# Selector-free attention for the groups from 6 on, and a new hand-written order of all steps

## The chip, the cores and the metric

The kernel runs on one core of a Trainium2 chip. The time is that of the device in microseconds (us), one launch, and the kernel before is given by the median of three runs. Five engines work from queues of their own, each in program order: PE (matrix multiply), DVE (vector), ACT (activation), POOL (GpSimd) and SP, which here only issues transfers. An engine goes on to its next instruction when the semaphores that this one needs have been raised, so one late instruction holds back all behind it on that engine.

## The reference

Linear attention with a feature map, followed by a two-layer MLP with an ELU in between. 8 batches of 8 heads, 576 positions, head size 64, 128 features; 4608 tokens of width 512; hidden width 2048.

```python
def phi(x):
    proj = np.einsum('bhsd,df->bhsf', x, w_phi)
    proj = proj - np.max(np.abs(proj), axis=-1, keepdims=True)
    return np.concatenate([np.exp(proj), np.exp(-proj)], axis=-1)
q_p, k_p = (phi(q), phi(k))
kv = np.einsum('bhsf,bhsd->bhfd', k_p, v)
z = np.sum(k_p, axis=2)
num = np.einsum('bhsf,bhfd->bhsd', q_p, kv)
den = np.einsum('bhsf,bhf->bhs', q_p, z)[..., None] + 1e-06
x = (num / den)            # then heads side by side: (4608, 512)
h = x @ w_in
g = np.where(h > 0.0, h, np.exp(np.minimum(h, 0.0)) - 1.0)
out = g @ w_out
```

With m the largest magnitude of a position's projection, the first half of its features is exp(proj - m) and the second exp(m - proj). So the two halves of a query's features carry different powers of exp(m), which do not cancel in the quotient, and m has to be applied somewhere.

## The kernel before

Four heads make a group (16 groups, two per batch). A group's k and q come in by a casting load (POOL queue, letters e, f, g for k, q, v), are transposed to feature-contraction layout (by PE for the first four groups, letters j to m; by a DMA transpose on the SP queue for the rest, letters n for k and o for q), and then run through these steps. A letter is a step of the order; a digit after it is the first PSUM bank it uses, a star puts it on the other of two engines.

- k side: A (`k_mm`, L267) three projections; B (`k_exp`, L278, ACT) both exponentials; C (`k_max`, L285, DVE) largest magnitude; D (`v_exp`, L295, ACT) and E, F (`v_scale`, `v_ones`, L304 and L313, POOL) scale v by the factor of each key; U (`kv_mm`, L477) and V (`kv_copy`, L487).
- q side: M (`m_mm`, L341) projects with positions on the partitions, N (`m_max`, L368, DVE) takes the largest magnitude. Then O (`m_split`, L394 and L395) splits it in two bf16 parts, P (`m_pe`, L401) transposes them, Q (`m_copy`, L406) copies them out of PSUM, and S (`q_mm`, L437) projects q again with features on the partitions; into the same banks L449 adds the maxima, by six matmuls with the 0/-1 selector matrix `sel` for each third. T (`q_exp`, L461, ACT) takes both exponentials.
- output side: W (`x_mm`, L526) multiplies by kv; both halves of the features add up in PSUM. X (`x_div`, L540, L541, L543, DVE) divides, and z (`x_dma`, SP queue) transposes the quotient into `xT`, the input of an MLP chunk, and into `xT_last`, which collects the ninth slot of 64 positions of all batches for the last chunk.
- MLP: nine chunks of 512 tokens. p (`h_mm`, L633) four matmuls of 512 columns; q (`h_exp`, L644, ACT); r (`h_min`, L649, POOL); s (`h_elu`, L653, DVE) writes `gT`; t (`o_mm`, L661) four matmuls of 512 columns into an output tile, four t to a tile; u (`o_copy`, L671) and v (`o_store`, L677).

No scheduler stands behind this: `ORDER` is one string of letters, and the loop at the end of the kernel pops, for each letter, the next argument of that step and issues its instructions. The order on every engine's queue, SP's and POOL's among them, is that of the string. `xT` has four buffers (`RING = 4`).

A second path is in the code and not taken: groups from `JOINED` on, and `JOINED` is 16. There, M makes ten places instead of nine (pieces of 4, 3 and 3), so that a query's maximum lies on the partition where its output row will be; w (`m_exp`) takes exp(m) and exp(2m) of it; S leaves the selector out; W writes the two halves of the features to separate banks in three pieces of 7, 7 and 6; x (`x_join`) multiplies the second half by exp(2m) and adds the first, R (`x_rec`) makes the reciprocal of the denominator, and y (`x_scale`) multiplies by it on POOL, or with a star on DVE. O, P, Q and X fall away. o issues two transposes of 64 partitions instead of one of 128.

Of the kernel before, what the change touches and what calls it, by code (L numbers as in the profile page):

```python
# [15 lines left out]


ORDER = """
eabeefgcj7dj6fkA0gk*CeA2A4CBj7CBl6Dkj1Bml0kDA6mEBM0CBA2ENBEBCl5l4BfmOBmhP7A0QM4BFES6NDBM2ETOCP5E
Q*TNU4FDFM6UBENj3V*S0kFEW4Tj7XU2hTUgkM4V*Y6NOM0Z*P7W2QNS4l7O*TXP6S0Q*Tl6mY3j2TZS4Tkj7mTW2kTp7XS0  # L20
qA4Tl6rsm*p3CTM6qNA0Bp2risBM6Cp3qp5qrl4Dsrm*Np2qp4qrsBA6Fsrp3CqqrBsrsEDsM4Bp2NM0Bp3NOM4qY7qrNp6r
W0eqZp5sFrsP7p4EqXQ*qS2rTsrS0sfM6Tsp5NETY4p3ZqEA6Tp2Cp4qrqU0BrsrsUqsBp5rVeS2qst7TrTA0p6CW2qsp4rB
stO*qXDrp6Bp5qsP1zW2qQrrsp4FsS0qXnp6Trp5EqzA2TtCrqEp1sDp0sBFtroEsBS4u*qp6EqTp7zU2TrrsUqsnqS4rV*r
p1ssW2zqTt7rsXop6A0qtTCrzM2sBW4NztBXp6M0qM2zA4NrtBgst1BNutCM2A6DM4NBFtO*fNBP3tQ*CM4S2t0u*TNTp7ED
S1qEA3S5TCtrTtEsToBU1FEp7TvBgA5UCqnO*p4V*rBW1szDp3qXvrtqsBW1rEp7sXp6qEA3u*qM1rnp5Brsp0qszBp7rNqp
6CzqrP2p1seqzsFp5rqDvrsp4qrsp7zqrsp6fsqvQ*rM0S2Esp5TNqt4rqrstTEsM0A2U6NFBrUO*BsS0tV*CTP7S5A2TotC
TW0QTt7XDBEW5zBS0XEtTzTA2S5CtTzu*BtTS0u*t4ToBM5tNTA2nM5BtNDBM0EA5tBCFp7EuNBU2FqOA0CUBnrp4VDzCM5q
p3NrBp2qsW0srqp7DsrgP6sp5qXQ*rp4qt6rszEsS0S2vTEp7Tzp5ETtqeTtfqM0qrS2NtrTosFTW0Frsp4EXp7qszrA0qU2
suUrvCM4V*p6szBW2Nqp7BXrp5qsp4rqsrA0qA2p6nsBrt7sBvOW4BCtzBXP1tqzDCrQ*A4S0EBzsM2TCtgTNFt6DBFu*EA0
S2BM4tfTCtETNtBEA2uM0U4eNBUBS6Vp1oTCA4Dp0TzFDp3qvqrp7qrvsBp6rsqW1sBrp0XqEnt3qsrtCEztsEW1zp7XrtO*  # L30
qsrM1M4u*p6sp3qNP7rp0qNQ*rt2sFS4M6TtNTtsqOp7rEsU3qS5A0rTtCTUsBS5Vp7Tou*Bp4vqW0qrP3p2vTQXrDp3zqsr
S0qst6zTrsp7TEszA4qS0CtzTrEsTM2ntNBFS0DA2ETtCoBt7EBW4gTtXFBU0zM2A4UNtV*vCuM0W2BzNtBXvt6uOzM0A2M4
NBtzNDP7tBEQCS0fA4TtBW2Tp7Xp1qCzrS2qt0u*EDzTstFBEvp7TFM4rqS2Np6ETosTU4rqUsA1rV*np3BsW4qCp7rteOqs
DP6rXtBp3uQszA1qM4S6NBzrp0TEsp5vCqEp4qTp3rBnrsW6qsp2qrXA0rp5Bszqp7sDrqp6CvFqrt4sBrzsqA2FS0sBrp5g
CtqsBtrETsS2M6Top5NETU0TM6UqNA2V*tODnCEW0up7BXrt6FqEszBP4W0DtQ*XFzEtzES0M2TtNrvTU4u*S0vM2UTNp6Tz
sV*M2S0NA4Tot7CTp3BA0tqCBrp2qsp5qrDp6rsqsBp4rqsW2qrtBXFrp5EszA0qM2sp6EBNzp4qrp3rsqOCtrqt5rsBsuP6
tsQ*M0A2S6NtTCDtTFEW0Bp7Xt6qzp4rsp1vqtrqzsBp7ru*ES2sqU4TrM0tNTUsA0S2Cp7VDtqEBp5u*O*TFp4rqp6srqTp
7rssP5W2Q*qt5XBrtqEszp4rW0zqA2p6CvtXDBEtqszp1Frp7rvsqEsut4zqrBtrvsU2sS0UTS5VTp7tqTrS0tTTp3u*TW5q
W0Xrp4st2zqsp7rXvtqsztrsp6zp7qtrqsp5rust6vqtrzsttp7p5qt4rqsp3rsp7qtrqsutrvsp6tt7uqtvrp5stqtrsp6t
5qp4rstqp6rsp3qp4rqstrqstrsp6t4qp3rsp2qp6rqsutrqvsp7rstqp6rsp3qup7rqvstrqsp6rsp5qt7rqsup3rvstqtr  # L40
stp6p5qp4rqst3rqstrsp6u*tqvp7rstqt6rusp5vp7qtrqsp4rsp5qp7rqstrqstrst5utvttt7utvttt6utvttt7u*tvtt
uv
"""


# [1 line left out]
def kernel(  # L47
# [178 lines left out]
    def new_t(name):  # L228
        return lambda: tpool.tile([P, NI, P], BF16, name=name + "T")
# [86 lines left out]
    def m_mm(n, c, bank=None):  # L316
        if n >= JOINED:
            v0, v1 = M_PIECES[c]
            pj = two_banks(bank).rearrange("p r (i f) -> p r i f", f=F)
            for v in range(v0, v1):  # L320
                for par in range(2):
                    hi, u = divmod(v, 5)
                    tpar, i0 = TILES[1][(2 * u + par) // 5][(2 * u + par) % 5]
                    assert tpar == par
                    rows = slice(par * D, (par + 1) * D)
                    nc.tensor.matmul(
                        pj[:, par, v - v0, :],
                        by_head(n)[rows, hi, i0 * D:(i0 + 2) * D],
                        w_sb[rows, :],
                        start=True,  # L330
                        stop=True,
                    )
            st["pm", n, c] = pj
            return
        own = min(n // FIRST, 1)
        p0, p1 = PIECES[own][c]
        pj = two_banks(bank).rearrange("p r (i f) -> p r i f", f=F)
        for j in range(p1 - p0):
            for par in range(2):
                rows = slice(par * D, (par + 1) * D)  # L340
                nc.tensor.matmul(  # L341
                    pj[:, par, j, :],
                    st["qT", n][rows, PLACE_OF[own][par][p0 + j], :],
                    w_sb[rows, :],
                    start=True,
                    stop=True,
                )
        st["pm", n, c] = pj

    def m_max(n, c):  # L350
        if n >= JOINED:
            v0, v1 = M_PIECES[c]
            mq = get(("mq", n), lambda: small.tile([P, 20], FP32, name="mx"))
            nc.vector.tensor_reduce(
                mq.rearrange("p (v r) -> p r v", r=2)[:, :, v0:v1],
                st["pm", n, c][:, :, 0:v1 - v0, :], axis=AX.X, op=ALU.max,
                apply_absolute_value=True,
            )
            return
# [8 lines left out]
        nc.vector.tensor_reduce(  # L368
            mq, st["pm", n, c][:, :, 0:p1 - p0, :], axis=AX.X, op=ALU.max,
            apply_absolute_value=True,  # L370
        )
# [37 lines left out]
    def q_mm(n, c, bank=None):  # L409
# [373 lines left out]
```

## Time and profile before

| | |
|---|---|
| median of 3 runs | 373.46 us (372.49 to 373.53) |
| the profiled execution, its own time | 373.46 us |
| its span, first to last instruction | 371.7 us |
| granted TensorE clock | 0.997 |
| PE busy | 349.8 us |
| ACT busy | 251.5 us |
| DVE busy | 244.7 us |
| POOL busy | 194.3 us |
| first matmul starts | 4.73 us |
| last matmul ends | about 367 us |
| DMA transposes of q, 12 | 1.31 us on the queue, 3.3 us to landing |
| DMA transposes of `xT_last`, 28 | 1.23 us on the queue, 3.1 us to landing |

The span is 1.76 us shorter than the time of that execution; this stands around the span and holds no instruction of the kernel. Rows of the profile give one instruction's duration from its start to its end; matmuls are pipelined, so a stream of them costs less per matmul than the row's mean.

### The profile page before, as it was taken

Reading aid. Unit: us, or ns where it says so; the run is one execution under the profiler, and the core shown is the slowest. Engines: PE = TensorE matmul, PEld = TensorE weight load, DVE = VectorE, ACT = ScalarE, POOL = GpSimd, SP = SyncE. Lnnn points to the kernel's source line nnn. Section 1 sums busy time; section 2 is a strip of 40 time slices with the busy share of each in tenths; the row PEclk is TensorE's granted clock in tenths of the full one; section 3 lists DMA queues with packets and bytes.
Section 4 is the critical chain, followed back from the end, with each engine's and each line's share of the span. In section 5 each row is a group of like instructions: output and inputs, shape, how many; then the busy total and the mean of one; then the engine's idle time right before and its main releaser. Section 6 shows DMA issues by size and latency. Waiting matters only on the chain.

```text
span 371.7 us, 9982 instructions
## 1 busy us (share of the span) xinstructions
PE 349.8 (94%) x4034; PEld 193.6 (52%) x4084; DVE 244.7 (66%) x425; ACT 251.5 (68%) x463; POOL 194.3 (52%) x307
## 2 busy tenths in 40 slices
PE   2798799999999999999999999999999999999994
PEld 1576576555465455554554555545555544444442
DVE  3968986867876868777767787777664632454400
ACT  2969798787789688955977898686566432453410
POOL 6762778267943775684544676464554332353400
PEclk9999999999999999999999999999999999999998
DMA  7997998689965699990679879620204212021223
GB/s 107 178 206 130 175 207 134 99 140 188 153 132 81 86 176 163 169 180 2 119 112 174 118 147 118 114 60 7 47 19 103 58 32 56 0 58 29 56 69 74
DMA packets 68158, 39.72 MB, mean 107 GB/s; under 512 B 48016, under 2 KB 62480, under 8 KB 68112
## 3 DMA queue, kind: packets, MB, share of 16 engines
q1 hardware_dynamic: 52176, 20.59, 31.8%
q0 software_dynamic: 15856, 18.35, 31.7%
q8 instruction: 32, 0.52, 0.6%
q14 instruction: 14, 0.11, 0.1%
q10 hardware_dynamic: 80, 0.13, 0.1%
HBM read 36.77 MB, written 9.44 MB: 124 GB/s over the span
## 4 chain that ended last, share of the span: by engine, by line
PE 82%; DVE 7%; ACT 3%; issue 3%; POOL 2%; DMA 1%; POOLq 0%; ACTq 0%
PE banks L661 32%; PE banks L633 29%; PE banks L477 5%; PE banks L526 5%; PE banks L437 3%; PE banks L341 2%; PE banks L267 2%; PE banks L449 2%; ACT EK L278 2%; DVE gT L653 2%; POOL e_sb L649 1%; DVE mk L285 1%; DMA kn<-in_k_dram 1%; DVE xp L543 1%; DVE mq L368 1%
## 5 line engine op out<-in xcount | busy, mean ns | idle before, releaser
L649 POOL TENSOR_SCALAR e_sb<-e_sb 128x512 f32<-128x512 f32 (+1 forms) x160 | 90.7, 571 | 115.2 <-ACT e_sb L644 106.4
L661 PE MATMUL banks<-w_out_sb,gT 128*128 128x512 bf16 x549 | 134.8, 379 | 2.6 <-issue 1.9
L653 DVE SCALAR_TENSOR_TENSOR gT<-e_sb,banks 128x512 bf16<-128x512 f32 (+1 forms) x160 | 98.3, 630 | 53.0 <-POOL e_sb L649 52.3
L644 ACT ACTIVATE e_sb<-banks 128x512 f32<-128x512 f32 (+1 forms) x160 | 88.0, 560 | 63.8 <-PE banks L633 57.5
L633 PE MATMUL banks<-xT,w_in_sb 128*128 128x512 bf16 (+1 forms) x554 | 124.0, 355 | 1.7 <-issue 0.3
L304 POOL TENSOR_TENSOR vs<-vn,em 128x576 bf16<-128x576 bf16 x64 | 73.0, 1153 | 32.2 <-ACT em L295 29.7
L633 PEld LDWEIGHTS <-w_in_sb 128*128 128x128 bf16 x640 | 58.3, 98 | 57.2 <-issue 0.6
L461 ACT ACTIVATE Eq<-banks 128x768 bf16<-128x768 f32 (+2 forms) x96 | 74.1, 815 | 14.8 <-PE banks L449 13.5
L661 PEld LDWEIGHTS <-gT 128*128 128x128 bf16 x576 | 52.7, 98 | 60.2
L278 ACT ACTIVATE EK<-banks 128x768 bf16<-128x768 f32 x96 | 75.6, 815 | 5.6 <-PE banks L267 2.5
L285 DVE TENSOR_REDUCE mk<-banks 128x6 f32<-128x768 f32 x48 | 45.7, 954 | 13.1 <-PE banks L267 8.9
L368 DVE TENSOR_REDUCE mq<-banks 128x6 f32<-128x768 f32 (+1 forms) x46 | 42.9, 941 | 17.0 <-PE banks L341 16.6
L543 DVE TENSOR_TENSOR xp<-banks,rec 128x640 bf16<-128x640 f32 (+2 forms) x32 | 26.4, 824 | 1.1
L526 PEld LDWEIGHTS <-Eq 128*128 128x128 bf16 x640 | 24.1, 98 | 5.7 <-issue 0.6
L526 PE MATMUL banks<-kv_sb,Eq 128*128 128x65 bf16 x640 | 25.5, 195 | 0.2
L477 PE MATMUL banks<-vs,EK 64*128 64x65 bf16 x1152 | 23.8, 194 | 0.3 <-ACT mT L406 0.2
L671 ACT COPY o_sb<-banks 128x512 f32<-128x512 f32 x21 | 12.3, 585 | 17.4 <-PE banks L661 16.6
L477 PEld LDWEIGHTS <-EK 64*128 64x128 bf16 x1152 | 21.1, 97 | 5.5 <-issue 3.5
L671 DVE COPY o_sb<-banks 128x512 f32<-128x512 f32 x15 | 10.3, 685 | 14.3 <-DMA out_dram<-o_sb 10.1
L341 PE MATMUL banks<-w_sb,qT 64*128 64x128 bf16 x288 | 16.7, 225 | 1.9 <-DVE gT L653 1.3
L267 PE MATMUL banks<-w_sb,kT 64*128 64x128 bf16 x288 | 16.9, 229 | 0.8 <-ACT kT L232 0.5
L437 PE MATMUL banks<-qT,w_sb 64*128 64x384 bf16 (+2 forms) x102 | 16.6, 328 | 0.7 <-DVE xp L543 0.5
(52 smaller groups left out, 186.6 us busy)
## 6 DMA issues: line engine op xcount, KB each, us to landing
out_dram<-o_sb SPq DMA_DIRECT2D x71, 128.0 KB, 2.4
kn<-in_k_dram POOLq DMA_DIRECT2D x7, 576.0 KB, 6.7
qn<-in_q_dram POOLq DMA_DIRECT2D x7, 576.0 KB, 7.5
vn<-in_v_dram POOLq DMA_DIRECT2D x7, 576.0 KB, 7.4
w_in_sb<-in_moe_w_in_dram POOLq DMA_DIRECT2D x2, 1024.0 KB, 10.6
w_out_sb<-in_moe_w_out_dram POOLq DMA_DIRECT2D x1, 2048.0 KB, 15.6
qn<-in_q_dram POOLq DMA_DIRECT2D x2, 288.0 KB, 7.2
vn<-in_v_dram POOLq DMA_DIRECT2D x2, 288.0 KB, 7.9
```

Of the source, the lines that this page charges most:

```text
L278: nc.scalar.activation(EK[:, sg, 6 * c:6 * c + 6, :].rearrange("p (i r) f -> p r i f", r=2), st["pk", n, c], ACT.Exp, scale=1.0 - 2.0 * sg,)
L285: nc.vector.tensor_reduce(mk[:, 6 * c:6 * c + 6].rearrange("p (i r) -> p r i", r=2), st["pk", n, c], axis=AX.X, op=ALU.max, apply_absolute ...
L304: nc.gpsimd.tensor_tensor(get(("vs", n), new_vs)[:, sg, r, 0:D], st["v", n // 2][:, 2 * (n % 2) + pr], st["em", n][:, sg, r].unsqueeze(2). ...
L368: nc.vector.tensor_reduce(mq, st["pm", n, c][:, :, 0:p1 - p0, :], axis=AX.X, op=ALU.max, apply_absolute_value=True,)
L461: nc.scalar.activation(Eq[:, sg, :, :, p0 * D:p1 * D].rearrange("p h r x -> p r h x"), st["pq", n, c][:, :, 0:(p1 - p0) * P].rearrange("p ...
L477: nc.tensor.matmul(kv[:, hi, pr, sg, :], EK[rows, sg, pr * NS + s, :], vs[rows, sg, pr * NS + s, :], start=(s == 0), stop=(s == NS - 1),)
L526: nc.tensor.matmul(pn[:, hi, x, :], Eq[:, sg, hi, par, i0 * D:(i0 + 2) * D], kv_sb[:, hi, pr, sg, :], start=(sg == 0), stop=(sg == 1),)
L633: nc.tensor.matmul(ph, w_in_sb[:, ct, jt * P:(jt + 1) * P], xT_of(ch)[:, ct, h0:h1], start=(ct == 0), stop=(ct == N_CT - 1),)
L644: nc.scalar.activation(e_sb, st["ph", ch, jt, h0], ACT.Exp)
L649: nc.gpsimd.tensor_scalar(e_sb, e_sb, 1.0, 0.0, op0=ALU.min, op1=ALU.max)
L653: nc.vector.scalar_tensor_tensor(gT[:, jt, h0:h1], st["e", ch, jt, h0], -1.0, st["ph", ch, jt, h0], op0=ALU.add, op1=ALU.max,)
L661: nc.tensor.matmul(po, st["gT", ch][:, jt, tt * P:(tt + 1) * P], w_out_sb[:, jt, :], start=(jt == 0), stop=(jt == N_JT - 1),)
```

## The change

`JOINED` goes from 16 to 6: ten of the sixteen groups (6 to 15) take the second path. The order is another string throughout. Nothing else changes: tiles, buffers, loads and the MLP's steps are the same.

```diff
 ORDER = """
-eabeefgcj7dj6fkA0gk*CeA2A4CBj7CBl6Dkj1Bml0kDA6mEBM0CBA2ENBEBCl5l4BfmOBmhP7A0QM4BFES6NDBM2ETOCP5E
-Q*TNU4FDFM6UBENj3V*S0kFEW4Tj7XU2hTUgkM4V*Y6NOM0Z*P7W2QNS4l7O*TXP6S0Q*Tl6mY3j2TZS4Tkj7mTW2kTp7XS0
...
+eabeeffj7k*gj6fA0kgBcA2dj7BeA4kBChl7Bhl6mBj1Cl7BkA2mDCM0Bl6ENBA4BECDm*FOA2ECm*P1Q*CBES6M0DTU4FNE
+TUOEDBM0VP7FBNEW4Q*XM2S0FEU6TNM4NUTOgj3V*P2M4iQkS0NS6TY3j2O*W4ZTl3XTP1l0TQm*kY5j7mW1Z*k*S3XA5Tp7
...
+qp4xDEnM0qp5NEvW2qtxeDtrnrsS0M2TgtRvswFp6NrTyp4sqRM0ru*qp5EsW2Nqp7ExS0qp6FTrp3rsqTrsp2rsqS0qyA4s
+op7TCrp6TrsqRU0BsrzqyA2sUBCrp7zV*sBW4W0zqxp6BrzDRS2qxp5Trt4TFsyqsS0A2TtRnCrTyM6vBNS0tETzsW6BExtT
...
 """
...
-    JOINED = 16
+    JOINED = 6
```

Steps of each kind in the two strings (kinds with the same number are left out):

| step | before | after |
|---|---|---|
| O, P, Q (`m_split`, `m_pe`, `m_copy`) | 18 each | 8 each |
| X (`x_div`) | 32 | 12 |
| W (`x_mm`) | 32 | 42 |
| w (`m_exp`) | 0 | 10 |
| x, R, y (`x_join`, `x_rec`, `x_scale`) | 0 | 30 each, 4 of the y on DVE |
| u with a star (copy of an output tile on DVE) | 15 | 17 |

At the head, the second half of q's first batch is loaded before v's first half, the whole q of the second batch before v's second half, and the two loads of `w_in` are issued earlier; the selector's two DVE steps (c, d) stand behind the first copies of the transposed k instead of before them, and the first of those copies is on ACT. PE changes between steps of 64 rows (A, M, S, U) and steps of 128 rows (all others) 170 times in the old string and 162 times in the new one.

More of the change, by code (lines that the diff above doesn't have):

```diff
@@ L18 @@
 ORDER = """
-eabeefgcj7dj6fkA0gk*CeA2A4CBj7CBl6Dkj1Bml0kDA6mEBM0CBA2ENBEBCl5l4BfmOBmhP7A0QM4BFES6NDBM2ETOCP5E
-Q*TNU4FDFM6UBENj3V*S0kFEW4Tj7XU2hTUgkM4V*Y6NOM0Z*P7W2QNS4l7O*TXP6S0Q*Tl6mY3j2TZS4Tkj7mTW2kTp7XS0
-qA4Tl6rsm*p3CTM6qNA0Bp2risBM6Cp3qp5qrl4Dsrm*Np2qp4qrsBA6Fsrp3CqqrBsrsEDsM4Bp2NM0Bp3NOM4qY7qrNp6r
-W0eqZp5sFrsP7p4EqXQ*qS2rTsrS0sfM6Tsp5NETY4p3ZqEA6Tp2Cp4qrqU0BrsrsUqsBp5rVeS2qst7TrTA0p6CW2qsp4rB
-stO*qXDrp6Bp5qsP1zW2qQrrsp4FsS0qXnp6Trp5EqzA2TtCrqEp1sDp0sBFtroEsBS4u*qp6EqTp7zU2TrrsUqsnqS4rV*r
@@ L24 @@
[L24 to L41, printed above, removed]
@@ L42 @@
-uv
+eabeeffj7k*gj6fA0kgBcA2dj7BeA4kBChl7Bhl6mBj1Cl7BkA2mDCM0Bl6ENBA4BECDm*FOA2ECm*P1Q*CBES6M0DTU4FNE
+TUOEDBM0VP7FBNEW4Q*XM2S0FEU6TNM4NUTOgj3V*P2M4iQkS0NS6TY3j2O*W4ZTl3XTP1l0TQm*kY5j7mW1Z*k*S3XA5Tp7
+p0TM1qNS3qrBrsp2TsCTA0p7qCl4Brj3k*sM5qp2NBrp3qsp6qmrBp7rsM4sqA0Nqp2rBrl3esY5qO*p4BsrZW6DCqEp5XP1
+p0qrQ*m*rp1EqsDM6sS2qNrp4TrsEp7TsY6sqM2Z*S0rNFTEU5sTM2p4NFqA0qUrBrsp3sCp7qV*t4rgO*BsA5S2BP1tQ*CT
+W0TtXnBW2qDA5rp1Bfsp0Xqp7BrtnsqCqrS2rp1TEsp6zu*qt5DsrTFsp7zqp4qrp3qFsp2rqrsS0qrstTEsoTp7rS3qEsA0
+Tzp6Cp2ETtqoqrU3BrsrUsezsA6V*tCBW2Bp4XW0BuXt7zqrA2M5sM0zBNtDBNp4EzM5qtNFvrfsM0A5CtO*BENP4t3BfDtC
@@ new lines @@
+Q*uEM0M4S6NEtTNTFU0OS4S6TUoTtVTW0TA4Xp2Bp7Cqnp6rqzsDW0rugp2qsvBrp7qvsp5rqXzp6rqsp4rqzsFrsA0qM2zp
+7sBrNp6EBqp5CqrnM2sqrp1srzp4NqEDP7p0svQ*qrsA2qrS6st5BFsETp1Trp4EBsS6qCtqrTtrsTsS2M0U6ToNUTA0VS2C
+TW6TtXBW2u*Bt4zXS0A5zTtCDtTzEBS2A0FtEToBt7u*DCtTEwA4zM2BECtBvNtFeBM0fuU2NBM6UNA0Bp5V*Ct7qp6BrsW2
+qp4xDEnM0qp5NEvW2qtxeDtrnrsS0M2TgtRvswFp6NrTyp4sqRM0ru*qp5EsW2Nqp7ExS0qp6FTrp3rsqTrsp2rsqS0qyA4s
+op7TCrp6TrsqRU0BsrzqyA2sUBCrp7zV*sBW4W0zqxp6BrzDRS2qxp5Trt4TFsyqsS0A2TtRnCrTyM6vBNS0tETzsW6BExtT
+zM2A0RM5NByt7DNtzBECA2S5FBtEoTCtTu*U0BA5zUCA2V*t4CnBtu*DBvEtBW0EvDW5wp7BxEtqFRp3xrfp2qseup6y*qrM
@@ new lines @@
+0S4rst7TEswp3TNp2qqrM0S4NFtTrsTetsqW0p6rxgp5qRsrM0qU3sUrNyp6V*RzS0qsp4TrW2qyotxTrp5usp3qsvrA0qS6
+p4RTzrsp2ysqvTCp5rqsW6zBrp3xqzt4BrqRA6S0sBtrosDytBsETW2CtTExzA5Dt7BFRzuA0CyM2tCEzBtNBFtEnwBM2U4N
+DzM0uEUNA2t7vBEVS0CntFTDW4vTEtxBW0FftRxyM2up6RNp7qW0rqA2xEp5Bt4syBqU0CrUrsM2V*p6NS0M2Tp7NqtsTrp5
+wgsqA0qrS2Cp6oTrstBRstByvqW0Tp7rxup5zqRrsS0A2Tp4sTnCW6qp1xzqrBp0rszDyp7qsqrS5zBp4rsqp3RqsrTW1rsp
+0qysDt7xqrzTtrsFM1sEA3S5BNtoFTtRCTyt2u*EBvA0M5wtNEBztBEzA3U5CBUDM0nV*EtNBW5zEwS0xt7TFTtCS0RA5DW3
+yTCtTExtuBEM0p4NBFW2qp6RxrU0qgsUurS2M4V*yosp7TNp6qTrM0p5NqvrS2sqA0p4Tszrp7RqCzTp6rsqp3sqrBW4rsp2
@@ new lines @@
+qsBrt7Dy*qA0xzp6rEtCqvp5srBzsFp4EBsvqM2A0RqtNrrp6ssM2qp5CDEtqNBt4rursW2Bp7xtqsrM0S2A5NFTtyswW0BR
+txyTt7BztuCvS0RS2DA4TFtCEzTtyDvBt6u*FEBzU0TUEvS4TVtETzW0TtExwtRU0yS2UTt7VTtW0p5xW2qp4u*rp1qRsp6r
+qxp5rqsW2rsqp4y*p1rszqRp6xrqztrqRvW2rsp0syp5qzxp4rqszp3rsqW1y*qp6Rsytxqrzp0ursp2srzqsp7rqsvt5rqs
+Rtrstystzt7ztttt6tttt4p3p2qp1rqsp0rqsp3rqsp2rqstrqu*p1rsvsp5qp3rqstrqsup2rvsp7qp5rqsp3rqstrqsp7r
+st5qtrsp3p7qp2rqsp1rqstrqsp7rstqu*ut3rvusp6vtqvtrsp7p6qtrqsp5rst7qtrstu*p6vtqp5rst4qu*p6rvsp7qtr
+qsp5rsp6qtrqsp7rsp5qtrqsp6rst7qu*trvsttt6u*tvttt7u*tvttt6u*tvttuv
```

## The prediction

> **What bounds the kernel now.** I read the page's totals and slices first, then the chain that ended last, then PE's rows in order of time, because the change takes work from PE and gives some to the others.
>
> ```profile
> PE 349.8 (94%) x4034; PEld 193.6 (52%) x4084; DVE 244.7 (66%) x425; ACT 251.5 (68%) x463; POOL 194.3 (52%) x307
> ...
> PE   2798799999999999999999999999999999999994
> ...
> DVE  3968986867876868777767787777664632454400
> ACT  2969798787789688955977898686566432453410
> ...
> PEclk9999999999999999999999999999999999999998
> ```
>
> PE stands at 9 from the sixth slice on (a slice is 9.3 us); only the first five, the head, and the last show idle time. The clock is full throughout, so it explains nothing.
>
> ```profile
> PE 82%; DVE 7%; ACT 3%; issue 3%; POOL 2%; DMA 1%; POOLq 0%; ACTq 0%
> PE banks L661 32%; PE banks L633 29%; PE banks L477 5%; PE banks L526 5%; PE banks L437 3%; PE banks L341 2%; PE banks L267 2%; PE banks L449 2%; ACT EK L278 2%; DVE gT L653 2%; POOL e_sb L649 1%; DVE mk L285 1%; DMA kn<-in_k_dram 1%; DVE xp L543 1%; DVE mq L368 1%
> ```
>
> The chain is PE to 82%, and no DMA transpose is on it: DMA appears with 1%, the first load of k. So room behind transposes is not what is short now. "Busy" can mislead for pipelined matmuls, so I take PE's rows by their starts (start, length, line, count):
>
> ```profile
> 102.49 0.33 PE L267 MATMUL banks<-w_sb,kT 64*128 64x128 bf16 x6
> 102.66 1.31 PE L477 MATMUL banks<-vs,EK 64*128 64x65 bf16 x72
> 103.81 0.32 PE L437 MATMUL banks<-qT,w_sb 64*128 64x384 bf16 x2
> ...
> 105.11 0.22 PE L401 MATMUL banks<-ident,mhl 128*128 128x128 bf16 x1
> 105.26 0.34 PE L437 MATMUL banks<-qT,w_sb 64*128 64x384 bf16 x2
> 105.43 0.33 PE L449 MATMUL banks<-mT,sel 64*128 64x128 bf16 x6
> 105.60 0.33 PE L267 MATMUL banks<-w_sb,kT 64*128 64x128 bf16 x6
> 105.86 1.04 PE L661 MATMUL banks<-w_out_sb,gT 128*128 128x512 bf16 x4
> 106.74 0.79 PE L526 MATMUL banks<-kv_sb,Eq 128*128 128x65 bf16 x20
> 107.36 1.02 PE L661 MATMUL banks<-w_out_sb,gT 128*128 128x512 bf16 x4
> ...
> 346.11 1.89 PE L633 MATMUL banks<-xT_last,w_in_sb 128*128 128x512 bf16 x8
> 347.83 1.03 PE L661 MATMUL banks<-w_out_sb,gT 128*128 128x512 bf16 x4
> ```
>
> Start to start: eight matmuls of 512 columns 1.72 (0.216 each); 72 of L477 1.15 (0.016); 20 of L526 0.62 (0.031); six projections or six selector matmuls 0.17 when 64-row work follows, 0.26 when 128-row work follows. So a change between the two kinds costs 0.1 (also at 105.11: one transpose takes 0.15 before 64-row work, of which some 0.055 is its own).
>
> With these the old string holds this PE work: p 124.5, t 124.4, U 18.4, W 19.8, A 7.7, M 7.7, S 15.4, transposes 6.1, 170 changes of kind 16.3; together 340. The last matmul ends at 367: 27 are lost, 4.7 ahead of the first matmul, some 17 in the first 50 us, only about 5 in the 317 behind. **The head waits for ACT, DVE and loads; from 50 us on PE sets the end.**
>
> The Trainium skill (Perfetto Trace Analysis, Identifying the Most-Contended Engine) speaks against this reading: it calls matmul busy time a poor measure and judges by weight-load busy, which is 52% here. By that rule PE has spare time and the change would save nothing, 373.5 less nothing; the starts, which follow each other without a gap, decide for me, and the saving is counted in full.
>
> **PE's part.** Ten groups leave out the selector: 30 times six matmuls of L449 at 0.17, -5.1. Ten transposes L401 at 0.055, -0.5. M gets ten places instead of nine, one pair more per group: ten times 0.053 (a third of 0.16), +0.5. W has 40 matmuls per group either way, S keeps its two of 384 columns. Eight changes of kind fewer, -0.8. Sum **-5.9**. All of it lies on the bound engine behind the head, so nothing hides it unless another engine takes over.
>
> **The other engines, per joined group.** The trace has no x, R, y or w; the nearest rows bound them:
>
> ```profile
> L543 DVE TENSOR_TENSOR xp<-banks,rec 128x640 bf16<-128x640 f32 (+2 forms) x32 | 26.4, 824 | 1.1
> ...
> L304 POOL TENSOR_TENSOR vs<-vn,em 128x576 bf16<-128x576 bf16 x64 | 73.0, 1153 | 32.2 <-ACT em L295 29.7
> ```
>
> An x instruction (455 or 390 elements, one operand in PSUM) lies between 0.56 (L653's 0.630 for 512, scaled) and 0.82 (L543 whole); I take L543 by elements, 0.59, so 1.17 for a pair. R is two small ones of 0.16 to 0.22 (L540, L541), 0.4. y on POOL lies between 0.57 (L649, one input, 512) and 1.15 (L304, two inputs, 576); scaled from L304, 0.90. w is two of 0.21 (L295). M's first piece has 1024 elements: N 1.23 (L368's 128x1024 form) for 0.95. So DVE gains 3.4 + 1.2 + 0.3 and loses two X at 1.2 and a bit of O and Q: about +2.2 a group, 22 in all; POOL +2.6 less O, 20 in all; ACT +0.4, 4 in all. Totals (DVE 267, ACT 256, POOL 215) stay far below PE's 334, so only stretches matter.
>
> **Stretches.** I laid PE's steps of each string end to end by the spacings above and summed, over stretches of 20 us of PE work, what the string gives the others. Behind 60 the old string never gives one engine more than 19.8 of 20. The new one stands out in three places. (a) From 100 to 120 the new string gives DVE 14 s (0.69), 3 C, 3 N, 4 x pairs, 5 R and a copy: 22.9, and ACT 19.7; the old one 15.4 each. PE would be held up by 2.9 if nothing stood ready; between p and the t that need its `gT` lie some 10 us at the median, so part is covered. I take 1.5, bounds 0 and 4.5 (the upper price of x adds 1.8 there). What is late then is s, behind it the bank that p or M wants. (b) From 20 to 60 ACT gets 40.8 for 40, the old string 36.3. ACT was idle for 6.2 of the 40 us from 10 to 50, which can take the 4.5; on the other side the new head lets the first exponential start before the first k maximum, where the old one waited 0.63 for it. I take +1.0, bounds -1.5 and +4.5. (c) From 180 to 200 ACT gets 20.1, DVE 19.7: +0.2, bounds 0 and 1. Together **+2.7**.
>
> **SP and the transposes.** Ten q transposes become two of 64 partitions, 256-byte pieces as before, so no more data: +1.25 of issue each, 12.5 on SP. From o to its M the new string leaves at least 8.0 of PE work (old 6.7); two issues (2.5) and a landing (3.1 for the 64-partition row, 3.3 for q) make 5.8. Cover 2.2; at the slowest landing seen, 10.3, M would be late by 4.8 and all p and t behind it on PE. From z to the first p of its chunk at least 7.2 (old 6.05). Priced at 0, as hidden behind PE's MLP work; bounds 0 and +4.8. The loads keep 5.7 or more before the n or o that needs them, the old string 6.0, against 6.7 to 7.9 to landing; SP waits there, PE does not: 0, the same bound. The other order of loads in the head (q's second batch before v's second half) delays v by one load of 576 KB at most, inside (b).
>
> The Trainium skill (SBUF — State Buffer, Who interferes with whom) has a rule against this change: a DVE instruction with two SBUF inputs and a GpSimd instruction that reads SBUF block each other for a whole instruction. R's first instruction and the four y on DVE are such. L395 on DVE is one too, and its nine took 175 to 181 ns with POOL busy half the time, so this trace shows no such wait and I add nothing; by the rule (an estimate from that page: five R in stretch (a), half of a POOL instruction each in about half of the cases) it would be some 1 us more.
>
> **Sum.** -5.9 + 2.7 = -3.2 against the profiled execution's 373.46, which is also the median: **370.3 us**.
>
> **Rivals.** *The stretches cost nothing*: 373.46 - 5.9 = 367.6. For it: the old stretch from 80 to 100 gives ACT 19.8 of 20, and PE still runs at 9 there. Against: nothing in the old string holds 22.9. Chance 0.24. *The saving is eaten up*: (a) and (b) at about twice my price, 373.5; the freed PE time turns into waits of PE for DVE. Chance 0.15. *Slower: x_join blocks DVE.* DVE waits for W's matmuls at the head of X now:
>
> ```profile
> DVE den L540 <- PE banks L526: 9.8, 13, 1.6
> ```
>
> 9.8 over 32 pieces, 0.31 each. The new string has 30 x pieces in the joined groups, each of which can wait for W and for w of ACT, with s, C and N queued behind it. If every piece costs PE the 0.31 on top of (a) to (c), it is 370.3 + 9.3 = 379.6; beyond 3.2 / 30 = 0.11 per piece the change is slower than before. For it: stretches where DVE is full have no time to catch up. Also for it: the shortest way from U to its W is 0.31 of PE work, 0.85 in the old string. Against: 20 X pieces with the same wait fall away, and at the median that way is 2.05 for 1.73. Taken with half of the pieces waiting, 375.0. Chance 0.22. That the selector is not left out is no rival: the sum of L449 follows from `JOINED`.
>
> **How the numbers follow.** Forecast 0.39, rivals 0.24, 0.15, 0.22. Two executions that differ by under 0.3% (1.1 us) can't be told apart; faster means below 372.3. Faster 0.39 + 0.24 = 0.63, same 0.15, slower 0.22. The likeliest case alone spans 368.5 to 372. The range of 8 in 10 takes in most of the first rival and the slower one up to its half price and 1 more: 366.8 to 376.
>
> **What would show it.** L449 at 108 matmuls for 288, L401 at 8. From 60 us to the end PE starts without gaps, except near 120 to 140 us, where DVE should stand above 9 and PE wait for gT or a maximum. At 60 us of time, PE's count of done steps tells (b). Wrong would be: waits of PE for `qT` or `xT` of a DMA, DVE idle for L526 by more than 15 us, or a head longer by more than 3.

## The result, and the profile after

The changed kernel takes **369.13 us** (median of four runs, 369.07 to 369.67) against 373.21 for the kernel before beside it (372.49 to 373.53): ratio 0.9897, 95% interval 0.9878 to 0.9915. The profiled execution is the one of 369.07, with a span of 367.3. Totals, slices and the chain's shares by engine of the kernel after, to be held against those of before:

```profile
PE 345.5 (94%) x3867; PEld 188.5 (51%) x3914; DVE 267.1 (73%) x470; ACT 253.4 (69%) x482; POOL 214.7 (58%) x323
...
PE   3797899999999999999999999999999999999995
...
DVE  2987977777896899877988797889748924544530
ACT  3888898868889689876986897896774504542400
...
PEclk9999999999999999999999999999999999999999
...
PE 80%; DVE 7%; ACT 4%; POOL 3%; issue 3%; DMA 2%; SPq 0%; POOLq 0%; DVEq 0%; ACTq 0%
```

PE lost 4.3 us of busy time and DVE gained 22.4, POOL 20.4 (busy time is the time in which an instruction of that engine runs); PE still stands at 9 from the sixth slice on, and the chain is still PE's. The groups of the second path (out<-in, shapes, count, busy and mean ns of one, idle time before them and what ended it):

```profile
L354 DVE TENSOR_REDUCE mx<-banks 128x6 f32<-128x768 f32 (+1 forms) x30 | 30.9, 1040 | 6.0 <-PE banks L326 5.3 <-PE banks L267 0.5
L555 DVE TENSOR_TENSOR xs<-banks,e 128x455 f32<-128x455 f32 (+1 forms) x30 | 18.0, 600 | 8.9 <-PE banks L510 6.6 <-ACT e L377 1.5 <-POOL xj L576 0.3
L560 DVE TENSOR_TENSOR xs<-banks,xs 128x455 f32<-128x455 f32 (+1 forms) x30 | 18.3, 610 | 1.1
L567 DVE SCALAR_TENSOR_TENSOR denj<-e,xs 128x7 f32<-128x7 f32 (+1 forms) x30 | 6.2, 206 | 0.3
L571 DVE RECIPROCAL recj<-denj 128x7 f32<-128x7 f32 (+1 forms) x30 | 5.9, 198 | 1.0
L576 POOL TENSOR_TENSOR xj<-xs,recj 128x448 bf16<-128x448 f32 (+1 forms) x26 | 23.3, 897 | 9.3 <-DVE recj L571 9.3
...
L449 PE MATMUL banks<-mT,sel 64*128 64x128 bf16 x108 | 6.4, 223 | 0.0
```

L449 has 108 matmuls left of 288. Where PE still loses time is read from stretches (the stretch, its length, then busy time and count of PE, PEld, DVE, ACT and POOL, granted clock, DMA share, GB/s). Before, then after:

```profile
0.00:50.00 50.00, 37.52 (x621) 28.36 (x623) 38.21 (x78) 36.93 (x73) 32.67 (x58) 1.00 0.99 163
...
140.00:150.00 10.00, 9.66 (x92) 4.88 (x92) 9.01 (x17) 8.43 (x18) 5.19 (x8) 1.00 1.07 144
```

```profile
0.00:50.00 50.00, 37.60 (x665) 29.14 (x666) 38.52 (x78) 39.03 (x78) 32.19 (x56) 1.00 1.06 173
...
140.00:150.00 10.00, 9.19 (x90) 4.44 (x89) 9.63 (x19) 9.13 (x19) 6.85 (x9) 1.00 0.61 91
```

The head gives PE the same 37.5 us of work, with 2.1 more of ACT in it: it got no longer. The stretch with the largest loss is 140 to 150, where DVE is at 9.63 of 10 and ACT at 9.13, and PE falls to 9.19.

Part of that fall is not real. These two traces lack some matmul records, 50 of 4084 before and 47 of 3914 after (the traces of experiments 1, 9, 10 and 12 have all), and a record that is missing at the head of a step looks like 0.16 of idle time. PE in that stretch, in the order of time (start, length, line, count; the wait ahead in brackets):

```profile
144.06 0.81 PE L661 MATMUL banks<-w_out_sb,gT 128*128 128x512 bf16 x3 [0.16 <-issue]
...
146.81 0.54 PE L510 MATMUL banks<-kv_sb,Eq 128*128 128x65 bf16 x12 [0.17 <-DVE mx L354]
...
149.31 1.67 PE L661 MATMUL banks<-w_out_sb,gT 128*128 128x512 bf16 x7 [0.16 <-issue]
```

A t has four matmuls, so the x3 and the x7 each lack one; the old kernel's 9.66 lacks one such record too. Read by the starts, three steps are late: S at 145.34 by 0.30 and A at 148.64 by 0.31, both for a bank that ACT's exponential (`q_exp`, L461) reads, and W at 146.81 by 0.33 for DVE's maximum (L354). All stalls of the stretch sum to some 1.0 there, and to some 0.7 in the old kernel: about 0.4 more.

The account by starts, as in the prediction, gives: PE's work laid end to end 340 before and 334.4 after (foretold: 334.1); stalls of the first 50 us 17.4 and 17.3; stalls behind them 4.1 and 5.5. The saving of 4.4 between the two profiled executions is thus about 5.6 less work, 0.1 less head, and 1.4 more of waits behind it. Some 0.4 of these lie from 140 to 150 us; the others are scattered, the next largest 0.5 from 100 to 110, ahead of the first x (121.5). These are single executions, and the runs of one kernel above differ by 0.6 to 1.0, so the 1.4 is a rough number.

### The profile page after: what moved, and what is told of

Read it like the earlier page. It is cut to its first block, busy times and chain, and to the rows that moved or that the text cites. A ratio compares the mean times of both kernels' runs of the same rounds, so it can differ in the third digit from the quotient of the medians.

```text
span 367.3 us, 9751 instructions
## 1 busy us (share of the span) xinstructions
PE 345.5 (94%) x3867; PEld 188.5 (51%) x3914; DVE 267.1 (73%) x470; ACT 253.4 (69%) x482; POOL 214.7 (58%) x323
## 4 chain that ended last, share of the span: by engine, by line
PE 80%; DVE 7%; ACT 4%; POOL 3%; issue 3%; DMA 2%; SPq 0%; POOLq 0%; DVEq 0%; ACTq 0%
PE banks L661 32%; PE banks L633 30%; PE banks L477 5%; PE banks L510 3%; PE banks L437 2%; PE banks L267 2%; PE banks L326 2%; DMA qn<-in_q_dram 2%; PE banks L526 2%; DVE gT L653 1%; ACT EK L278 1%; POOL vs L304 1%; POOL e_sb L649 1%; DVE mk L285 1%; ACT e_sb L644 1%
## 5 line engine op out<-in xcount | busy, mean ns | idle before, releaser
L649 POOL TENSOR_SCALAR e_sb<-e_sb 128x512 f32<-128x512 f32 (+1 forms) x160 | 90.7, 572 | 100.5 <-ACT e_sb L644 98.1
L653 DVE SCALAR_TENSOR_TENSOR gT<-e_sb,banks 128x512 bf16<-128x512 f32 (+1 forms) x160 | 96.5, 626 | 41.7 <-POOL e_sb L649 41.4
L633 PE MATMUL banks<-xT,w_in_sb 128*128 128x512 bf16 (+1 forms) x557 | 122.7, 355 | 2.0 <-DVE mq L368 0.5
L304 POOL TENSOR_TENSOR vs<-vn,em 128x576 bf16<-128x576 bf16 x64 | 72.9, 1153 | 22.2 <-ACT em L295 17.2
L461 ACT ACTIVATE Eq<-banks 128x768 bf16<-128x768 f32 (+2 forms) x96 | 74.2, 815 | 13.1 <-PE banks L437 9.0
L354 DVE TENSOR_REDUCE mx<-banks 128x6 f32<-128x768 f32 (+1 forms) x30 | 30.9, 1040 | 6.0 <-PE banks L326 5.3
L576 POOL TENSOR_TENSOR xj<-xs,recj 128x448 bf16<-128x448 f32 (+1 forms) x26 | 23.3, 897 | 9.3 <-DVE recj L571 9.3
L555 DVE TENSOR_TENSOR xs<-banks,e 128x455 f32<-128x455 f32 (+1 forms) x30 | 18.0, 600 | 8.9 <-PE banks L510 6.6
L671 ACT COPY o_sb<-banks 128x512 f32<-128x512 f32 x19 | 11.1, 589 | 14.8 <-DMA out_dram<-o_sb 13.2
L510 PEld LDWEIGHTS <-Eq 128*128 128x128 bf16 x400 | 16.2, 97 | 7.3 <-issue 1.1
L560 DVE TENSOR_TENSOR xs<-banks,xs 128x455 f32<-128x455 f32 (+1 forms) x30 | 18.3, 610 | 1.1
L671 DVE COPY o_sb<-banks 128x512 f32<-128x512 f32 x17 | 11.6, 684 | 9.9 <-PE banks L661 9.9
L510 PE MATMUL banks<-kv_sb,Eq 128*128 128x65 bf16 x400 | 17.1, 194 | 0.3 <-DVE mx L354 0.3
```

Of the source, the lines that this page charges most:

```text
L304: nc.gpsimd.tensor_tensor(get(("vs", n), new_vs)[:, sg, r, 0:D], st["v", n // 2][:, 2 * (n % 2) + pr], st["em", n][:, sg, r].unsqueeze(2). ...
L354: nc.vector.tensor_reduce(mq.rearrange("p (v r) -> p r v", r=2)[:, :, v0:v1], st["pm", n, c][:, :, 0:v1 - v0, :], axis=AX.X, op=ALU.max, a ...
L461: nc.scalar.activation(Eq[:, sg, :, :, p0 * D:p1 * D].rearrange("p h r x -> p r h x"), st["pq", n, c][:, :, 0:(p1 - p0) * P].rearrange("p ...
L510: nc.tensor.matmul(pn[:, sg, v - v0, :], Eq[:, sg, hi, par, i0 * D:(i0 + 2) * D], kv_sb[:, hi, pr, sg, :], start=True, stop=True,)
L633: nc.tensor.matmul(ph, w_in_sb[:, ct, jt * P:(jt + 1) * P], xT_of(ch)[:, ct, h0:h1], start=(ct == 0), stop=(ct == N_CT - 1),)
L649: nc.gpsimd.tensor_scalar(e_sb, e_sb, 1.0, 0.0, op0=ALU.min, op1=ALU.max)
```

## The experiments

"The new kernel" and "the old kernel" are those after and before the change; each ratio is to the old kernel timed on the same chip with it. The new kernel was not timed again beside the experiments: "above the new kernel" is a difference of medians to 369.13, and the ratios give up to 0.8 us less for the slower kernels and up to 0.7 more for the faster ones.

**1. The selector's PE time put back.** The new kernel, in which the ten groups again run the 180 selector matmuls, on a tile of zeros, so that they add nothing.

```diff
...
-        for j in range(w if n < JOINED else 0):
+        for j in range(w):
...
-                    st["mT", n][rows, 0, :],
+                    st["mT", n][rows, 0, :] if n < JOINED else zero_m[rows, :],
...
```

> The new kernel with the selector's matmuls put back into S of the groups from 6 on, as dead work: six per third, against a tile of zeros, into the banks that S writes anyway. 180 matmuls of L449's kind, priced at 0.17 per six, 5.1 us. My theory (the saving is PE time on the bound engine, the order itself is worth nothing): 369.1 + 5.1 = 374.2, so level with the kernel before, ratio 1.000 to 1.005. Rival (the new order is what is faster, and PE has time to spare, as the weight loads' 51% would say): 369 to 370, ratio 0.99.

Measured: 373.42 us, ratio 0.9998 (0.9983 to 1.0014). Against the new kernel that is +4.3 by the medians and +3.8 by the ratios (1.01%), for 5.1 priced. With these 180 matmuls back, the gain of the change is gone to within 0.2%. By the starts PE's work is some 5 us longer in this trace, as priced, and the stalls behind the head some 0.8 shorter. The Trainium skill (Perfetto Trace Analysis, Identifying the Most-Contended Engine) judges PE's headroom by weight-load busy together with the share of the peak arithmetic. Read by the weight loads alone, as the prediction read it, PE should have had time to spare. It had none: the weight-load share is 52% with the 180 matmuls and 51% without them, and they cost 3.8 to 4.3 us.

**2. Only the selector left out, in the old order.** Would the old kernel have got the gain without the second path? The maxima of the queries of ten groups are missing from the result.

```diff
-                    stop=n >= JOINED,
+                    stop=n >= 6,
...
-        for j in range(w if n < JOINED else 0):
+        for j in range(w if n < 6 else 0):
```

> The kernel before, in its old order, with the selector's matmuls left out of S in the groups from 6 on (the maxima are then not subtracted there); M, O, P, Q and X stay, and no x, R, y or w is added. 180 matmuls less, 5.1 us by the row. My theory: 373.2 - 5.1 = 368.1, ratio 0.986, so the old order with this one saving is as fast as the new kernel or faster. Rival (the order matters by itself): the old order gives back part of it as waits of PE, 371 or more, ratio 0.994 or above.

Measured: 372.88 us (369.53 to 374.29), ratio 0.9968 (0.9934 to 1.0001): 0.4 us gained by the medians and 1.2 by the ratio, instead of some 4, and a wide spread. The theory on record (368.1) missed; this is the rival's outcome. PE in the order of time (start, length, line, the wait ahead of it in brackets) shows where one part went:

```profile
192.03 1.89 PE L661 MATMUL banks<-w_out_sb,gT 128*128 128x512 bf16 x8
...
196.85 0.34 PE L341 MATMUL banks<-w_sb,qT 64*128 64x128 bf16 x6 [2.93 <-DMA qT<-qn]
```

The transpose for this M was issued at 187.45, which is 1.30 earlier than in the old kernel's trace (188.75), and M still waited 2.93 for it. SP's row here, and the old kernel's:

```profile
187.45 1.71 SPq L251 DMA_TRANSPOSE qT<-qn  x1
...
188.75 1.37 SPq L251 DMA_TRANSPOSE qT<-qn  x1
```

The transfers that ran in that stretch of kernel 2 (queue, kind, count, KB, us to landing):

```profile
qT<-qn SPq DMA_TRANSPOSE x1, 9.4
vn<-in_v_dram POOLq DMA_DIRECT2D x1, 576.0 KB, 7.5
qn<-in_q_dram POOLq DMA_DIRECT2D x1, 576.0 KB, 5.9
```

The same transpose landed in 5.8 us in the old kernel and takes 9.4 here. In the old kernel M came 7.2 us after the issue; here it would have come after 6.5 without the wait. So the missing selector took 0.7 of the room, and the larger part of the wait, 2.2, is the slow landing itself, which the old kernel's way would not have covered either. Why it was slow stays open: the two loads of 576 KB stand in that stretch of both traces (7.5 and 5.9 to landing here, 9.8 and 7.5 in the old kernel). PE's other longer waits (1.9 for `mhl`, 1.3 for gT) are in the old kernel's trace too.

**3. Fewer changes of kind.** The new kernel with 16 small moves of PE's steps, p or t past steps of 64 rows or the other way round, so that PE changes 130 times between 64-row and 128-row steps instead of 162. One of the moves, a t ahead of an M:

```diff
-...DBNp4EzM5qtNFvr...
+...DBNp4EztM5qNFvr...
```

> The new kernel with PE's steps moved by one neighbour so that steps of 64 rows stand together: 16 small moves behind the head, each by at most 0.37 us of PE work, bring the changes between 64-row and 128-row steps from 162 to 130. All other queues keep their order. By the price of 0.1 per change: -3.1 us, 366.0, ratio 0.981. If a change costs nothing by itself (the rows' 0.1 is only the start of another kind of matmul, paid once more elsewhere): 369.1, ratio 0.989. If the moves cost waits of other engines: between, or above 369.

Measured: 388.91 us, ratio 1.0415 (1.0359 to 1.0472). PE's work did shrink by some 2.3 us (last matmul at 380.7, less 4.7 ahead of the first and 43.9 of stalls, leaves 332.1 by the starts, against 334.4), but the stalls grew by about 21. The waits of PE in this kernel (what waited, for what: us in total, times, longest), followed by two stretches of its rows:

```profile
PE banks L326 <- DVE mx L354: 3.0, 3, 1.2
PE banks L477 <- DVE mx L354: 2.8, 2, 1.9
PE banks L437 <- DVE mx L354: 2.7, 4, 1.0
PE banks L267 <- ACT Eq L461: 2.4, 2, 1.5
```

```profile
119.08 0.56 PE L326 MATMUL banks<-w_sb,qT 64*128 64x128 bf16 x14
121.51 0.75 PE L477 MATMUL banks<-vs,EK 64*128 64x65 bf16 x36 [1.87 <-DVE mx L354]
...
149.75 0.34 PE L267 MATMUL banks<-w_sb,kT 64*128 64x128 bf16 x6 [1.50 <-ACT Eq L461]
151.65 0.50 PE L437 MATMUL banks<-qT,w_sb 64*128 64x384 bf16 x2 [1.33 <-ACT Eq L461]
```

Each waits for the reader of a PSUM bank (DVE's maximum, ACT's exponential) to let the bank go. The expectation called the moves small, at most 0.37 us, by the length of the 64-row steps. But what these steps were moved past is longer: a p or t has 0.86 us of PE work. Twelve steps of 64 rows (A, M and S) are asked for 0.86 to 1.7 us earlier than in the new kernel, and ten come as much later. In the new kernel's trace A, S and M start at the median 0.2 to 0.4 us after the last semaphore that they wait for was raised. Of the twelve earlier steps, ten wait here, 0.5 to 1.5 us each (S at 151.65 is one), together 10 of the 21. The others follow from them or from the later steps: behind the M of the move shown, A waits 1.05 for M's maximum.

**4. x_join's multiplication twice.** The slower rival, doubled: the new kernel with the first instruction of each x done a second time.

```diff
+        nc.vector.tensor_tensor(
+            xs, pn[:, 1],
+            st["e1", n][:, 1, v0:v1].unsqueeze(2).to_broadcast((P, v1 - v0, D + 1)),
+            op=ALU.mult,
+        )
         nc.vector.tensor_tensor(xs, pn[:, 0], xs, op=ALU.add)
```

> The new kernel with x_join's multiplication done twice: 30 more DVE instructions of 0.60 us, 18.0 us of DVE work (267 to 285 of 367 busy). My theory: DVE sets the end only in its full stretches (two to three of 20 us); the addition is 3.6 us in each 20 us of the joined part, so it costs 2 to 5 us, 371 to 374. Rival, the slower case of the prediction (DVE's queue is what PE waits for at every x piece): 0.60 for each of 30, up to 18 us, 380 or more. If DVE has room everywhere: 369.1.

Measured: 381.50 us, ratio 1.0212 (1.0183 to 1.0241), 12.4 above the new kernel. DVE's busy time rose from 267.1 to 284.1, so each added us cost 0.73 (0.69 by the ratios). That is not the 2 to 5 us of the theory on record but the rival's outcome, 380 or more. The first two lines of its chain:

```profile
PE 61%; DVE 26%; ACT 4%; issue 4%; DMA 2%; POOL 2%; SPq 0%; DVEq 0%; POOLq 0%; ACTq 0%
PE banks L666 25%; PE banks L638 21%; DVE gT L658 5%; PE banks L477 4%; DVE xs L560 4%; DVE xs L555 4%; DVE xs L565 3%; DVE mk L285 3%; PE banks L267 2%; PE banks L437 2%; PE banks L526 2%; DVE mx L354 2%; PE banks L510 2%; DMA kn<-in_k_dram 1%; ACT EK L278 1%
```

DVE's share of the chain goes from 7% to 26% (gT and the three instructions of x are 5, 4, 4 and 3 of it), though it is busy in only 75% of the span. DVE's busy share of 73% was no reserve here.

**5, 6. Room behind the q transposes in the old order.** Kernel 5 is experiment 2 with a third buffer of the transposed tiles and each q transpose but one issued 2.2 to 2.9 us of PE work earlier; kernel 6 is the old kernel with that room and nothing else. The edit common to both, with one of the places:

```diff
-...Xnp6Trp5EqzA2Tt...
+...Xnp6Trp5oEqzA2Tt...
...
-    tpool = ctx.enter_context(tc.tile_pool(name="tpool", bufs=2))
+    tpool = ctx.enter_context(tc.tile_pool(name="tpool", bufs=3))
```

> The run e2_old_no_selector once more (old order, selector left out of S in the groups from 6 on), with three instead of two buffers for the transposed k and q, and with every DMA transpose of q but one issued 2.2 to 2.9 us of PE work earlier in the string. In e2 PE waited 2.9 us once for a q transpose that landed late, and its times spread from 369.5 to 374.3. Theory now (the old order had just enough room behind the transposes; 5 us less PE work brings M nearer to its transpose, and the wait eats the saving): with room the wait goes, 369 to 369.7, ratio 0.988 to 0.990, spread under 1.5 us. Rival (the old order waits for ACT or DVE instead, the q transpose being one accident of the profiled execution): it stays at 372 to 373, ratio 0.997.

> The kernel before, selector and all, with the same three buffers and the same earlier q transposes. Its trace shows no PE wait for a transpose. Theory: no gain, 373.2, ratio 0.998 to 1.002; room is worth something only once PE work is gone. Rival (room is what the new order brings, with or without the selector): 370 or less, ratio 0.992 or below.

Measured: kernel 5 370.02 us, ratio 0.9904 (0.9885 to 0.9923), against 0.9968 without the room. The transpose that was late is issued earlier, and the wait of M for it is gone:

```profile
182.08 1.31 SPq L251 DMA_TRANSPOSE qT<-qn  x1
```

This one now landed in 3.2 us, with 12.9 to its M; another took 10.2 to landing and had 11.1.

Kernel 6: 375.10 us, ratio 1.0042 (1.0019 to 1.0065): room alone gains nothing and costs 0.4%. Its trace has one wait of 1.9 us of an x matmul that no semaphore of the profile explains; the cause of the 0.4% stays open. So room was worth nothing with the selector in place, and about 2.4 us (0.64%) without it. The third buffer and the earlier issue were not tried apart.

**7, 8. How much room the new order has.** The new kernel with its q transposes issued 2 and 4 us of PE work later. One of the places, for 7 (the second o of the old line comes behind the cut in the new one):

```diff
-...rstTEsoTp7rS3qEsA0Tzp6Cp2ETtqoqrU3B...
+...rstTEsTp7rS3qEsA0Tzp6Cp2ETtoqqrU3B...
```

> The new kernel with every DMA transpose of q issued 2 us of PE work later, so that the shortest way from it to its M falls from 8.0 to 6.0. The prediction put the cover at 2.2 at the usual landing: 369.1 to 369.5 then, ratio 0.989 to 0.990. If landings of up to 10 us are common, waits of 2 us at several of the twelve groups: 372 and more, with a wide spread.

> The same by 4 us of PE work: shortest way 4.0 against two issues of 1.25 and a landing of 3.1 to 3.3, 5.8. Six groups have ways of 8.0 to 9.9 and would each make PE wait for up to 1.8 us: +4 to +10, 373 to 379. If nothing moves (369.1), the transposes have more cover than worked out.

Measured: 2 later 369.47 us, ratio 0.9889 (0.9874 to 0.9903), no cost; 4 later 376.03 us, ratio 1.0070 (1.0047 to 1.0092), 6.9 above the new kernel. In the second it is one long wait, not many short ones. SP's row and PE's row of it:

```profile
117.52 3.54 SPq L246 DMA_TRANSPOSE qT<-qn  x2
...
126.86 0.61 PE L326 MATMUL banks<-w_sb,qT 64*128 64x128 bf16 x8 [4.78 <-DMA qT<-qn]
```

From issue to the waiting matmul 9.3 us go by, where the two issues and a landing at the median came to 5.8; the first of the two halves took 9.3 to landing. The time lies in the expected range, the mechanism is not the expected one: no other group waits, and one with 5.2 us from issue to M had its halves in 1.0 early. At the usual landing the cover is thus larger than the 2.2 of the sum; what broke was the cover for a slow landing. In the new kernel the slowest half took 8.6, with 14.5 to its M.

**9, 10. DVE work taken away.** Kernel 9 is the new one without x_rec (y multiplies by a constant; the quotient isn't formed); kernel 10 takes the reciprocal of the denominator directly and leaves out 1e-6 times exp(m) in the ten groups.

```diff
-        nc.vector.scalar_tensor_tensor(
-            den, st["e1", n][:, 0, v0:v1], 1e-6, st["xs", n, part][:, :, D],
-            op0=ALU.mult, op1=ALU.add,
-        )
-        nc.vector.reciprocal(st["rec", n, part], den)
+        nc.vector.reciprocal(st["rec", n, part], st["xs", n, part][:, :, D])
```

> The new kernel without x_rec: y multiplies by a constant, so the denominators are left out in the groups from 6 on. 60 small DVE instructions less, 30 times 0.206 and 30 times 0.198, 12.1 us of DVE work. They hold no PSUM bank themselves. Theory (the new kernel's remaining waits behind the head sum to some 5 us, 1 to 1.5 us more than before, in the stretches full of DVE work): 368 to 368.8, ratio 0.985 to 0.988. Rival (DVE is a bound beside PE throughout, as the 12.4 us for 18.0 of the doubled join suggest): 12.1 times 0.69 back, 361 to 363.

> The new kernel with the 1e-6 times exp(m) left out of the joined groups' denominators, the reciprocal reading x_join's column directly: 30 DVE instructions of 0.206 less, 6.2 us of DVE work. Theory as for e9, half of it: 368.5 to 369.0, ratio 0.987 to 0.989. Rival: 364 to 366.

Measured: kernel 9 368.22 us, ratio 0.9854 (0.9829 to 0.9878); kernel 10 368.27 us, ratio 0.9857 (0.9830 to 0.9884). Twelve us of instructions less, or six, give the same: 0.9 by the medians, 1.5 to 1.6 by the ratios, which the intervals barely tell from none. Kernel 10 in the stretch of the loss, to be held against 9.19 above:

```profile
140.00:150.00 10.00, 9.83 (x87) 4.45 (x83) 9.49 (x16) 9.51 (x18) 7.48 (x10) 1.00 0.55 92
```

This trace has all its records, so of the 0.64 between 9.19 and 9.83 the two missing ones make 0.32. By the starts the waits of W and A (0.33 and 0.31) are gone with three DVE instructions fewer, the wait of S (0.30) stays, and just ahead of the stretch PE waits 0.39 for gT, where the new kernel has 0.16. From 130 to 150 some 0.4 is gained, and some 0.6 in all behind the head. Six more us off DVE (kernel 9) gave nothing more.

**11. Every y on DVE.** The new kernel with all 30 multiplications by the reciprocal on DVE instead of 4, by a star at each y of the order.

> The new kernel with all 30 x_scale on DVE instead of 4: 26 instructions of 0.62 to 0.68 more there, 17 us (267 to 284, as in e4_join_twice), 23.3 us less on POOL. Unlike the doubled join none of them reads PSUM. If what cost 12.4 us in e4 is the time that a bank stays taken: at most 4 us, 369 to 373. If it is DVE's time as such: 12 us again, 379 to 382. If two-input SBUF instructions on DVE are held up by POOL's (median 0.62 and 0.85 at worst now), their mean rises above 0.75.

Measured: 375.96 us, ratio 1.0060 (1.0038 to 1.0082), 6.8 above the new kernel. The y on DVE took 666 ns each; DVE's busy time rose by 15.0 and POOL's fell by 20.3. The cost is 0.45 per us of DVE (0.41 by the ratios), against 0.73 in experiment 4, and lies between the two outcomes on record (at most 4, or 12). The instructions of experiment 4 read PSUM and so also keep W's banks, those here don't. That this is the reason for the difference was not tried by itself.

**12. The same as 10, and 1e-6 left out in the first six groups too.**

```diff
-        nc.vector.tensor_scalar_add(den, pn[:, :, :, D], 1e-6)
-        nc.vector.reciprocal(rec, den)
+        nc.vector.reciprocal(rec, pn[:, :, :, D])
```

> e10 with the addition of 1e-6 left out of X in the first six groups as well: 12 DVE instructions of 0.163 less, 2.0 us of DVE work, all in the head and just behind it, where PE loses most of its time (some 17 us in the first 50) and DVE is at 8 to 9 of 10. If the head waits for DVE: up to 1.5 us less than e10, 366.8 to 367.8, ratio 0.982 to 0.985. If the head waits for ACT and the loads: as e10, 368.3, ratio 0.985 to 0.987.

Measured: 367.93 us (367.20 to 368.19), ratio 0.9854 (0.9838 to 0.9871), the fastest of all, 1.2 below the new kernel by the medians and not to be told from kernels 9 and 10. The twelve steps X lie before 110 us and lose one DVE instruction of 163 ns each; no effect on the time can be told, as expected if the head waits for ACT and the loads.

## Why the prediction was right, and where its sizes were off

**Forecast and range.** 370.3 was foretold, 369.1 measured: inside the range, and nearly half way between the forecast and the first rival (367.6).

**What bounds the kernel.** Right, and shown by experiment 1.

**PE's part, -5.9.** Measured -5.6 by the starts. The selector's term was priced at 5.1; restored, it brought some 5 back as PE work and 3.8 to 4.3 as time. For the eight changes of kind at 0.1, experiment 3 gives 0.07 each (32 changes fewer, some 2.3 us less work), and shows that work saved by moving a step is not time saved.

**The others' prices.** The x pair was priced at 1.17 and took 0.600 and 0.610, R 0.4 and took 0.40, y 0.90 and took 0.897. Little of the error comes from here.

**Stretch (b), the head: the term that was mis-sized.** "I take +1.0" and it was about 0. The trace after has 39.03 us of ACT in the first 50 for 36.93 before, and PE did 37.60 for 37.52; from 50 to 80 us, where the rest of this stretch lies, the stalls are 0.4 in both traces. The reason given for the lower bound (ACT's idle time of 6.2 could take the 4.5) was the better one. This 1.0 is nearly all of the 1.2 by which the forecast missed. Single executions show it only roughly: PE's wait for the first load of q alone is 0.7 in this trace and 2.6 in that of experiment 1.

**Stretch (a) and (c).** +1.5 and +0.2 were foretold and 1.4 came behind the head, but the sum agrees better than its parts: only some 0.4 lies where (a) was found, the rest in small waits elsewhere that had no term. That they add up to nearly the same is luck. The place was near: foretold for 120 to 140 us of time, where PE stands at 9.95 and 9.75 (9.89 twice before), and found from 140 to 150, just behind PE's work at 120 (120 and the 22 of stalls ahead of it). The mechanism was right in part: DVE is at 9.63, and with DVE work taken away (experiment 10) two of the three waits go. But two of the three are for ACT's exponential and none is for gT; the chain that ended last runs through DVE from 140.1 to 145.6 and from there through ACT. Of the 2.9 us by which DVE was to hold PE up if nothing stood ready, the 1.5 taken was still too much for this stretch.

**SP and the transposes, 0.** Right for this kernel: no PE wait for `qT` or `xT` behind the head, and 2 us later costs nothing (experiment 7). But the sentence that room behind transposes "is not what is short now" was true of the old kernel alone. Experiments 2 and 5 show that it becomes short when the selector is gone and the old order is kept; then 0.4 to 1.2 us of the gain are left, and more room brings it back to 3.6 (0.96% of 373.78). The new order has more (the least from issue to M is 9.3 us in the trace after and 6.8 in that of before), and with 4 us less of it one slow landing takes the saving away (experiment 8). The trace of before couldn't show the shortage. The cover of 2.2 was too low a figure for the usual landing; a slow one, the bound of the prediction, is what experiment 8 met.

**"Totals stay far below PE's 334, so only stretches matter."** This step failed as a rule. DVE's total stayed far below PE's in experiments 4 and 11 as well, and each us added to it cost 0.73 and 0.45. It held only downwards: taking 6 or 12 us away gave no more than 1.6. A reading that fits experiments 3 and 4, though no run tests it by itself: the order lets a bank or an operand come free just before PE wants it, so that every engine with work between two PE steps is part of that path, whatever its share.

**The rivals.** *The stretches cost nothing*: its 367.6 would be a ratio of 0.984, outside the measured interval, and the stalls behind the head did grow, by about 1.4. *The saving is eaten up*: no. *x_join blocks DVE*: DVE did wait for W ahead of x, 6.6 us over 30 pieces (0.22 each, 0.31 foretold), but no row of PE waits for x behind the head; presumably the idle time lay where DVE had slack. Experiment 4 shows that the mechanism is there and how near: 0.57 us more per x is enough to cost PE 0.41 for each of the 30 pieces.

**The rule on SBUF.** The Trainium skill (SBUF — State Buffer, Who interferes with whom) says that a DVE instruction with two SBUF inputs contends with a GpSimd instruction that reads SBUF. The prediction took nine rows of L395 as evidence against it and added nothing. That reading was wrong: at the start of eight of the nine no POOL instruction was running, and at the ninth only a step of a load (L201), so they could not show the wait. The trace after shows it in R's first instruction (shortest, median, longest ns):

```profile
L567 DVE SCALAR_TENSOR_TENSOR denj<-e,xs x30: 155/168/595, 126.3 to 294.3; 128x7 f32<-128x7 f32 x20, 128x6 f32<-128x6 f32 x10
```

Fifteen of the 30 met no POOL instruction and took 155 to 170 ns. Eight took 188 to 595, and each of these began while POOL ran L649, L576 or L304; seven ended 19 to 24 ns after that POOL instruction did. The eighth, 240 ns, met two in a row. In experiment 11, behind the 1153 ns of L304, one took 1122. So the trace agrees with the page. The mean of 206 less the median of 168, times 30, is 1.1 us in the whole kernel; the estimate by the page was 1 us in stretch (a) alone, where one instruction (at 144.08, 479 ns) lost 0.3. That one is on the chain from 140 to 150, and experiments 9 and 10 take it away.

**Not tried.** The second path in the old order by itself. So what the new order alone is worth stays open; experiment 5 shows that the old order with room and without the selector reaches the same ratio (0.9904 for 0.9897).

## What to carry to other kernels

Where an engine's rows start without gaps, work taken from it was worth most of its start-to-start time (3.8 to 4.3 of 5.1 us here), but only where the transfers and bank releases that this work covered still came in time: count that cover again after the cut, against a slow landing and not the usual one. A busy share of 70% on a second engine was no slack in an order cut to measure: adding to it cost 0.4 to 0.7 of each us, taking 6 or 12 us from it gave at most 1.6 back. Swaps in a hand-written order that look free by instruction cost need not be: twelve steps asked for 0.9 to 1.7 us earlier met banks not yet released, and the kernel lost 20 us. And before busy times of two traces are compared in a stretch, count the records: two missing ones made half of the gap between 9.19 and 9.83.

## What the runs showed of the hardware

The transposing transfer of one q tile took from 3.2 to 10.3 us to landing in the old kernel, and up to 11.8 in kernel 5; what made the long ones long was not found. The median (3.3 and 4.2) was no measure for the room that it needs. A DVE instruction with two SBUF inputs of 7 elements per partition took 155 to 170 ns when no POOL instruction ran beside it and up to 595 (1122 in experiment 11) when one did, ending some 20 ns after it. A change between 64-row and 128-row matmuls cost PE about 0.1 us by the spacing of starts, and 0.07 by the sum of experiment 3.
